# RWKV-7 attention and a SoLU layer: the mean of w_out summed at other places, and other shares of the last two inverses

## Chip, cores and metric

The kernel runs on one core of one Trainium2 chip. The metric is the device time of one execution in microseconds. A core has TensorE (PE, matrix products into PSUM), VectorE (DVE), ScalarE (ACT), GpSimd (POOL), SyncE (SP, used here only to issue DMA), and 16 DMA engines. Each engine works through its own queue in order and waits on semaphores for the others.

## What is computed

The reference is an RWKV-7 recurrence over 4 batches, 8 heads, 768 tokens and head dimension 40, followed by a SoLU layer over 3072 tokens (320 to 1024 to 320). Cut to what matters:

```python
for t in range(S):                                   # attention, per batch and head
    y[:, :, t] = einsum('bhd,bhde->bhe', rt, state)
    Sa = einsum('bhde,bhe->bhd', state, at)
    state = state * wt[:, :, None, :] - einsum('bhd,bhe->bhde', Sa, bt) + einsum('bhd,bhe->bhde', vt, kt)
h = x @ w_in                                         # x: y as (3072, 320)
solu = h * softmax(h)
ln = (solu - mean(solu)) / sqrt(var(solu) + 1e-06) * g_ln
out = ln @ w_out
```

The weights come as 64-bit floats and are turned into 32-bit floats on the chip. Instead of subtracting the mean of solu from every row, the kernel subtracts from `w_out` (with g_ln folded in, `w2`) its mean over the 1024 rows. This mean is made once.

## The kernel before

The 768 tokens are cut into 12 chunks of 64. The two batches of a pair share 128 partitions, so there are N = 24 chunks of work, numbered i. The main loop (L815) runs one pass per i, from -1 to 27; such a pass is called a slot here. A slot holds work of several chunks at once: the early part of chunk i+5 (`front`, `norm`), the recurrence of chunk i (`solved`, `read`, `leave`), the preparation of chunk i+1 (`scores`, `flip`, `couple`, `close`), and the SoLU layer of chunks i-1 to i-4 (`hidden`, `exped`, `folded`, `output`). The order of all instructions on all five engines is the order in which the Python code emits them; no scheduler moves any.

Four things matter around the change.

**The inverse.** Within a chunk the recurrence needs the inverse of a triangular matrix, made for two chunks at a time by `invert`, a generator. Inverse n serves chunks 2n and 2n+1 and is begun in slot 2n-4. It is a chain of 30 steps on VectorE, each one product (L428, `prod`) and one subtraction (L430, `uu`) over the whole of `u`. `some(k)` runs k steps; each slot calls it at four places with the numbers of `shares`, or else of a default: (3, 5, 4, 5) in even slots, (0, 5, 4, 4) in odd ones. The four places are: at the slot's start; behind `hidden(m - 2, ((0, 1),))` and ahead of `front_b`; ahead of `couple`; and behind `carried`, ahead of `leave`. In the last place the newest inverse is left alone in the slot that begins it. When the last step is done, SP writes the result to DRAM (L436, `uu_dram`), and `bring(i + 1)`, at the start of slot i, loads it for chunk i+1 into `tu` and `uh` (L449, L451).

**From inverse to coupling.** `flip` (L457) transposes `tu` on VectorE, `couple` multiplies it on TensorE (`py`), ScalarE scales the result (`wy`), `close` multiplies again (`pz`), and `read` opens `pyo`. `norm` (product `pnt`) and `answered` (product `pl`) lie between `couple` and `close`; VectorE masks their results into `nt` and `lu`, both at L375. `leave` reads `pyo` on VectorE into `x` (L619) and `tot` (L634, L636).

**PSUM.** There are three pools. `banks` (two buffers) holds, in turn, pu, ps, py, pnt, pl, pz, pyo and px of each slot (no pnt from slot 19 on), so that each of them waits until the last but one has been read: pz for nt, pyo for lu, pu for x and tot. `bank` (two buffers) holds the transposes, pcum, po and pmean. `ps2` has one buffer, `h`, for the hidden layer; in slot 2 it is used only near the end.

**The weights.** In slots -1 to 4 the weights are split from 64-bit words (`split`, L182 to L195: VectorE, then three ScalarE instructions, then VectorE). `w2` has 8 chunks of 128 rows. When chunks are there, TensorE sums them with a constant matrix of 2^-10 (`mean_of`), ScalarE copies the sum to `mean` (L231), and later calls carry it on by adding it through the identity (L227). A 128x320 product in this type is two passes of TensorE. Slot 2 sums chunks 0 to 3 and slot 3 chunks 4 and 5, both behind `spreadof`; the third sum, chunks 6 and 7, stands at the end of slot 3, and `centred` subtracts the mean in slot 4 (LAG is 1, so the code's `i == 1 + LAG` is slot 2).

Of the kernel before, what the change touches and what calls it, by code (L numbers as in the profile page):

```python
# [9 lines left out]
FP32 = mybir.dt.float32  # L10
# [7 lines left out]
P = 128  # L18
# [6 lines left out]
LAG = 1  # L25
# [23 lines left out]
def kernel(  # L49
# [18 lines left out]
    nc = tc.nc  # L68
    B, H, S, D = r.shape
    DM = H * D  # L70
    DFF = moe_w_in.shape[1]
# [13 lines left out]
    ps2 = ctx.enter_context(tc.tile_pool(name="ps2", bufs=1, space=PSUM))  # L85
# [10 lines left out]
    def c_(name):  # L96
        lo, hi = where[name]
        return cst[:, lo:hi]

    ident, tri = c_("ident"), c_("tri")  # L100
# [31 lines left out]
    w2 = const.tile([P, NF, DM], FP32, name="w2")  # L132
# [3 lines left out]
    def banks(name):  # L136
        return ps1.tile([P, 2, 512], FP32, tag="banks", name=name)

    def bank(name):
        return ps3.tile([P, 512], FP32, tag="bank", name=name)  # L140
# [56 lines left out]
    begun = []  # L197
# [23 lines left out]
            nc.scalar.mul(out=x, in_=pg[:, 0:NF], mul=2.0 ** y)  # L221


    def mean_of(lo, hi, begun=None):
        t = bank("pmean")
        if begun is not None:
            nc.tensor.matmul(t[:, 0:DM], lhsT=ident, rhs=begun, start=True, stop=False)  # L227
        for c in range(lo, hi):
            nc.tensor.matmul(t[:, 0:DM], lhsT=c_("mean"), rhs=w2[:, c, :], start=begun is None and c == lo, stop=c == hi - 1)
        mean = two.tile([P, DM], FP32, tag="osb", name="mean", bufs=1)  # L230
        nc.scalar.copy(out=mean, in_=t[:, 0:DM])  # L231
        return mean
# [7 lines left out]
    def half(p):  # L240
        return slice(C * p, C * p + C)
# [6 lines left out]
    def in_turn(tile_of, some=units):  # L248

        lots = {}  # L250
        for u in some:
            lots.setdefault(tile_of(*u), []).append(u)
        lots = list(lots.values())
        return [lot[n] for n in range(max(map(len, lots))) for lot in lots if n < len(lot)]

    def mm(o, lhsT, rhs, start=True, stop=True):
        nc.tensor.matmul(o, lhsT=lhsT, rhs=rhs, start=start, stop=stop, skip_group_check=True)  # L257
# [10 lines left out]
    def heads(ap):  # L268
        return ap.rearrange("p (h d) -> p h d", d=D)
# [13 lines left out]
    def ok(i):  # L283
        return 0 <= i < N
# [12 lines left out]
    def load_values(i):  # L297
        if not ok(i):
            return
        d = st[i]  # L300
        d["lv"] = two.tile([P, H, W2], FP32, tag="lv", name="lv", bufs=3)
        d["raw_r"] = two.tile([P, H, D], FP32, tag="raw_r", name="raw_r")
        load(d["lv"][:, :, C:], v, i)
        load(d["raw_r"], r, i, nc.gpsimd)
# [9 lines left out]
    def logged(i):  # L314
        lw = st[i]["lw"] = two.tile([P, DM], FP32, tag="lw", name="lw", bufs=1)
        nc.scalar.activation(out=lw, in_=st[i]["raw_w"].rearrange("p h d -> p (h d)"), func=AF.Ln)

    def decay(i):
        if not ok(i):
            return  # L320
        d = st[i]
        if "lw" not in d:
            logged(i)
        t = (bank("pcum") if i > 5 else ps2.tile([P, DFF], FP32, tag="h", name="h"))[:, 0:DM]
        nc.tensor.matmul(t, lhsT=c_("cum"), rhs=d["lw"], start=True, stop=True)
        nc.scalar.activation(out=ei_t[0][:, :, 0:D], in_=heads(t), func=AF.Exp)
        inv = d["inv"] = two.tile([P, DM], FP32, tag="inv", name="inv", bufs=4)
        nc.scalar.activation(out=inv, in_=t, func=AF.Exp, scale=-1.0)
# [10 lines left out]
    def turned(name, x):  # L339
        t = bank("p" + name)  # L340
        for j in range(4):
            nc.tensor.transpose(out=t[0:W2, j * P:(j + 1) * P],  # L342
                                in_=x[:, 2 * j:2 * j + 2].rearrange("p a b -> p (a b)")[:, 0:W2], identity=ident)
        return t[0:W2].rearrange("p (j b t) -> p b j t", j=4, b=2)
# [9 lines left out]
    def decay_turned(i):  # L354
        if not ok(i):
            return
        ex = st[i]["ex"] = ex_t[i % (AHEAD + 2)]
        nc.scalar.copy(out=ex[0:W2, :, :, 1:], in_=turned("ei", ei_t[0]))
# [9 lines left out]
    def front_b(i):  # L368
        if not ok(i):
            return  # L370
        d = st[i]
        d["bT"] = kept("bT", turned("b", d["kb"][:, H:]))
# [67 lines left out]
    def bring(i):  # L440
        if not ok(i):
            return
        d = st[i]
        d["tu"], d["uh"] = tu_t[i % 2], uh_t[i % 2]
        n, at = divmod(i, GRP)
        src = inverse[n].rearrange("(e a h x) c t -> e a h x c t", e=2, a=GRP, x=2)
        for x in range(2):
            queue = nc.sync if i or not x else nc.scalar
            queue.dma_start(out=d["tu"][C * x:C * x + Q, :, Q:2 * Q], in_=src[0, at, :, x].rearrange("h c t -> c h t"))  # L449
        for x in range(2):  # L450
            nc.sync.dma_start(out=d["uh"][C * x + Q:C * x + C], in_=src[1, at].rearrange("h x c t -> c (h x) t"))  # L451
# [7 lines left out]
    def couple(i):  # L459
        if not ok(i):  # L460
            return
        d = st[i]
        t = banks("py")
        for u in in_turn(lambda p, q, g, h: (p ^ h, p)):
            p, q, g, h = u
            j = 2 * q + g
            x = half(p ^ h)
            mm(t[half(p), h, j * Q:j * Q + Q], d["nt"][x, h, j], d["tu"][x, 4 * h + j, 0:Q])
        nc.scalar.activation(out=wy[:, :, :, 0:Q], in_=t[:, :, 0:4 * Q].rearrange("p h (j c) -> p h j c", j=4),  # L469
                             func=AF.Copy, scale=c_("neg_hi"))  # L470
# [170 lines left out]
    def left(i):  # L641

        if not ok(i):
            return
        x, xT = st[i]["x"], st[i]["xT"]
        for h in range(2):
            at = C * h
            nc.gpsimd.dma_start(out=xT[3 * D:P, h], in_=x[at:at + P - 3 * D, 2])
            for to in (Q * h, C + Q * h):
                nc.gpsimd.dma_start(out=xT[to:to + Q, 2], in_=x[at + P - 3 * D:at + D, 2])  # L650
# [82 lines left out]
    def some(n, kept=0):  # L733
        while len(steps) > kept and n:
            if next(steps[0], steps) is steps:
                steps.pop(0)
            else:
                n -= 1
# [72 lines left out]


    shares = {-1: (0, 2, 3, 9), 0: (4, 5, 3, 4), 1: (0, 6, 4, 5), 2: (4, 4, 3, 4), 3: (0, 5, 4, 4), 4: (6, 1, 4, 6)}
    narrowed = {-1: (0, 1, 0), 0: (0, 1, 1), 1: (1, 0, 2), 2: (0, 1, 2), 3: (1, 0, 1)}
    for i in range(-1, N + 3 + LAG):  # L815
        j, m = i + AHEAD, i - LAG
        pieces = shares.get(i, (0, 5, 4, 4) if i % GRP else (3, 5, 4, 5))
        some_weights = narrowed.get(i, (0, 0, 0))
        if i >= 1:
            bring(i + 1)  # L820
        if i >= 0:
            load_values(i + 2)
        narrow(0, pieces[0])

        solved(i)
        if i >= 0:
            scores(i + 1)
        if i >= 0:
            load_keys(j + 3, "w")
        load_keys(j + 2, "bak")  # L830

        stated(i)
        front(j)
        hidden(m - 2, ((0, 1),))
        if i == 3 + LAG:
            centred(mean)
        narrow(some_weights[1], pieces[1])
        front_b(j)
        if ok(j + 2):
            logged(j + 2)  # L840
        decay_turned(j + 1)
        hidden(m - 2, ((1, 1),))
        flip(i + 1)
        highest(m - 2)
        scaled(j + 1)
        left(i - 1)
        decay(j + 2)
        output(m - 3, 0)

        some(pieces[2])  # L850
        couple(i + 1)
        exped(m - 2)
        norm(j)
        answered(i)
        weighed(m - 2)
        spreadof(m - 2)
        if ok(j) and j % GRP == GRP - 1:
            begin_inverse(j // GRP)
        if i == 0:
            turn_g()  # L860
        if i == 1 + LAG:
            mean = mean_of(0, 4)
        if i == 2 + LAG:
            mean = mean_of(4, 6, mean)
        output(m - 3, 1)

        close(i + 1)
        read(i, True)
        carried(i + 1)
        narrow(some_weights[2], pieces[3], ok(j) and j % GRP == GRP - 1)  # L870
        by_value(i + 2)
        if ok(m - 1):
            hidden(m - 1, ((2, 0), (2, 1)))
        fence()
        read(i, False)
        driven(i + 1)
        leave(i)
        begin_narrow(narrowed.get(i + 1, (0,))[0])
        folded(m - 2)
        hidden(m - 1, ((0, 0),))  # L880
        attend_kv(i + 2)
        hidden(m - 1, ((1, 0),))
        attend_r(i + 2)
        if i == 2 + LAG:
            mean = mean_of(6, NF, mean)
# [30 lines left out]
```

## Time and profile before

| | |
|---|---|
| three runs, median | 621.12 us |
| three runs, lowest and highest | 618.76 and 623.91 us |
| profiled execution, its own time | 617.47 us |
| profiled execution, span from first to last instruction | 615.7 us |
| mean granted clock of TensorE over the span | 0.938 |
| PE, DVE, ACT, POOL busy | 547.3, 448.7, 265.6, 257.7 us |
| inverse, L430 and L428 on VectorE | 102.1 and 97.6 us, 360 instructions each |

The page names each instruction by engine, line and operation, output first ("nt<-pnt"). A timeline's row has the start and the length in microseconds, and in brackets the idle time of the engine before it, with what ended that idle time. The chain of waits follows the work back from the last instruction. PEld is the loading of weights into TensorE. In the copies quoted here, a row with "x8" stands for eight instructions merged.

By the trace, slots 2, 3 and 4 begin with pu at 108.71, 136.46 and 160.38 us. From then on a slot takes 21 to 23 us (the second half of po starts at 170.69, 193.48 and 215.02 us in slots 4, 5 and 6). Slots 17, 18, 19 and 20 have their py at 451.09, 471.76, 492.71 and 512.13 us.

### The profile page before, as it was taken

The page shows a single profiled execution, that of the slowest core. Times are in us where ns is not written, and L with a number is a line of the kernel's source. Part 1 is how long each engine was busy: PE and PEld are TensorE (multiplying, and loading weights), DVE is VectorE, ACT ScalarE, POOL GpSimd, SP SyncE. Part 2 cuts the span into 40 slices and gives each one's busy share as a digit, 9 for nine tenths or more (in the row PEclk, how much of TensorE's full clock was granted, in tenths as well). Part 3 has the DMA queues.
Part 4 walks back from the last instruction along what each step waited for, and adds up shares of the span by engine and source line. Part 5 has one row for each costly group of instructions (what it writes and reads, how often), then busy time and mean ns, then how long its engine had stood idle before and what let it go on. Part 6 is the DMA issues. An engine that isn't in the chain of part 4 may idle for free.

```text
span 615.7 us, 26656 instructions
## 1 busy us (share of the span) xinstructions
PE 547.3 (89%) x11453; PEld 397.4 (65%) x11453; DVE 448.7 (73%) x1262; ACT 265.6 (43%) x548; POOL 257.7 (42%) x424
## 2 busy tenths in 40 slices
PE   4555587689899999999999999999999999999994
PEld 3334476566576777777777677777777676676652
DVE  4797978979968869868868868688698688443431
ACT  4434455454443544454454445444433343342221
POOL 3462272472452472473365355534624631322200
PEclk9666767789999999999999999999999999999998
DMA  8986895664445454564565574564532612310100
GB/s 166 156 157 132 176 176 107 139 137 84 82 105 98 94 118 94 97 118 99 94 122 97 95 127 97 111 110 82 109 56 53 122 44 44 65 35 26 28 19 21
DMA packets 213901, 59.93 MB, mean 97 GB/s; under 512 B 199120, under 2 KB 208952, under 8 KB 213784
## 3 DMA queue, kind: packets, MB, share of 16 engines
q1 hardware_dynamic: 195512, 33.78, 32.5%
q0 software_dynamic: 11568, 19.78, 13.9%
q10 hardware_dynamic: 6704, 4.67, 2.7%
q8 instruction: 90, 1.47, 1.0%
q14 instruction: 27, 0.22, 0.1%
HBM read 40.10 MB, written 13.37 MB: 87 GB/s over the span
## 4 chain that ended last, share of the span: by engine, by line
PE 71%; DVE 15%; DMA 4%; issue 3%; ACT 3%; SPq 1%; POOL 1%; ACTq 0%; DVEq 0%; POOLq 0%
PE po L723 16%; PE h L257 15%; PE pyo L257 7%; DVE prod L428 4%; DVE uu L430 4%; PE pu L257 4%; PE plnT L712 4%; PE ps L257 3%; PE px L257 3%; PE py L257 2%; PE pl L257 2%; PE pz L257 2%; PE pst L505 2%; PE pr L342 1%; PE pei L342 1%
## 5 line engine op out<-in xcount | busy, mean ns | idle before, releaser
L257 PE MATMUL h<-w_in,xT 128*128 128x512 f32 (+1 forms) x288 | 123.0, 610 | 0.0
L723 PE MATMUL po<-w,lnT 128*128 128x320 f32 x384 | 112.7, 438 | 0.5 <-ACT lnT L713 0.5
L430 DVE TENSOR_TENSOR uu<-uu,prod 128x30 f32<-128x30 f32 (+4 forms) x360 | 102.1, 284 | 12.4
L428 DVE TENSOR_TENSOR prod<-blk,uu 128x30 f32<-128x30 f32 (+4 forms) x360 | 97.6, 271 | 9.6
L723 PEld LDWEIGHTS po<-w,lnT 128*128 128x128 f32 x384 | 71.0, 190 | 32.6 <-issue 4.1
L401 POOL DMA_DIRECT2D nt_dram<-nt x20 | 18.9, 943 | 120.0 <-DVE nt L375 98.5
L375 DVE TENSOR_TENSOR psi<-ps,cst 128x512 f32<-128x512 f32 x24 | 16.6, 690 | 66.6 <-PE ps L257 66.6
L701 POOL TENSOR_TENSOR rs<-c,mhalf 128x1 f32<-128x1 f32 x24 | 13.5, 561 | 112.1 <-DVE c L700 103.2
L650 POOL DMA_DIRECT2D xT<-x x96 | 48.7, 512 | 0.0
L257 PEld LDWEIGHTS h<-w_in,xT 128*128 128x128 f32 (+1 forms) x288 | 37.4, 189 | 9.2 <-issue 8.1
L670 DVE TENSOR_REDUCE nmax<-h 128x1 f32<-128x1024 f32 x24 | 28.6, 1193 | 18.6 <-PE h L257 18.6
L412 POOL DMA_DIRECT2D blk<-nt_dram x46 | 36.6, 802 | 10.8 <-issue 6.8
L257 PE MATMUL pyo<-lv,kb 64*64 64x104 f32 x768 | 37.8, 266 | 2.2
L257 PEld LDWEIGHTS pyo<-lv,kb 64*64 64x64 f32 x768 | 23.9, 140 | 20.9 <-issue 20.8
L638 POOL TENSOR_TENSOR st<-tot,ex 104x160 f32<-104x160 f32 x44 | 21.8, 512 | 36.6 <-DVE tot L634 23.5
L257 PE MATMUL pyo<-lu,kb 64*64 64x104 f32 x768 | 36.7, 258 | 0.0
L469 ACT ACTIVATE wy<-py,cst 128x256 f32<-128x256 f32 x24 | 11.4, 473 | 56.2 <-PE py L257 56.2
L280 POOL DMA_DIRECT2D raw_r<-in_r_dram x48 | 33.9, 709 | 0.0
L727 ACT ACTIVATE osb<-po,rs 128x320 f32<-128x320 f32 x24 | 12.7, 527 | 48.5 <-PE po L723 32.9
L554 ACT COPY x<-px 128x320 f32<-128x320 f32 x24 | 10.2, 425 | 54.1 <-PE px L257 54.0
L678 ACT ACTIVATE e<-h,nmax 128x1024 f32<-128x1024 f32 x24 | 26.6, 1108 | 14.3 <-DVE nmax L670 14.3
L684 DVE TENSOR_TENSOR e<-h,e 128x1024 f32<-128x1024 f32 x24 | 29.2, 1217 | 4.6 <-ACT e L678 4.6
(128 smaller groups left out, 1162.6 us busy)
## 6 DMA issues: line engine op xcount, KB each, us to landing
blk<-nt_dram POOLq DMA_DIRECT2D x46, 128.0 KB, 4.4
nt_dram<-nt POOLq DMA_DIRECT2D x20, 256.0 KB, 3.5
raw_w<-in_w_dram SPq DMA_DIRECT2D x48, 80.0 KB
a<-in_a_dram SPq DMA_DIRECT2D x48, 80.0 KB
raw_r<-in_r_dram POOLq DMA_DIRECT2D x48, 80.0 KB, 3.1
lv<-in_v_dram SPq DMA_DIRECT2D x48, 80.0 KB
out_dram<-osb ACTq DMA_DIRECT2D x24, 160.0 KB
raw_b<-in_b_dram SPq DMA_DIRECT2D x44, 80.0 KB
```

Of the source, the lines that this page charges most:

```text
L257: nc.tensor.matmul(o, lhsT=lhsT, rhs=rhs, start=start, stop=stop, skip_group_check=True)
L280: queue.dma_start(out=x[half(p), :, 0:D], in_=ap[2 * bp + p, :, ci * C:(ci + 1) * C, :].rearrange("h t d -> t h d"))
L412: queue.dma_start(out=nb[home:home + Q], in_=blocks[n][:, Q * e:Q * e + Q, Q * e:Q * e + Q])
L428: nc.vector.tensor_tensor(out=t, in0=nb[:, j:j + 1, j + 1:Q].to_broadcast([P, n_c, m]), in1=u[:, 0:n_c, j:j + 1].to_broadcast([P, n_c, m]) ...
L430: nc.vector.tensor_tensor(out=u[:, 0:n_c, j + 1:Q], in0=u[:, 0:n_c, j + 1:Q], in1=t, op=ALU.subtract)
L638: nc.gpsimd.tensor_tensor(out=to3(old), in0=to3(tot[0:W2]), in1=ex[:, :, 2 * q:2 * q + 2, C:].to_broadcast([W2, 2, 2, D]), op=ALU.mult)
L650: nc.gpsimd.dma_start(out=xT[to:to + Q, 2], in_=x[at + P - 3 * D:at + D, 2])
L670: nc.vector.tensor_reduce(out=nmax, in_=d["h"], axis=AX.X, op=ALU.max, negate=True)
L678: nc.scalar.activation(out=e, in_=d["h"], func=AF.Exp, bias=d["nmax"], accum_out=d["esum"])
L684: nc.vector.tensor_tensor(out=d["e"], in0=d["h"], in1=d["e"], op=ALU.mult)
L712: nc.tensor.transpose(out=t[:, j * P:(j + 1) * P], in_=d["e"][:, f * P:(f + 1) * P], identity=ident)
L723: nc.tensor.matmul(d["out"][:, 0:DM], lhsT=d["lnT"][:, f, :], rhs=w2[:, f, :], start=f == 0, stop=f == NF - 1)
```

## The change

The function `mean_of` is split in three: `mean_part` adds chunks to a given PSUM tile, `mean_kept` copies the tile to `mean`, `mean_of` carries an earlier sum on in a new tile. In slot 2 the first sum covers chunks 0 to 2 instead of 0 to 3; it is made in a tile of `h`'s pool, chunks 0 and 1 ahead of `decay_turned` (pei), chunk 2 behind `left` and ahead of `decay` (pcum), followed by the copy on ScalarE. In slot 3 the second sum covers chunks 3 to 5 instead of 4 and 5 and stands ahead of `couple` (py) instead of behind `spreadof`. The third sum (6 and 7) stays. `shares` gets entries for slots 17 to 20, the slots that hold the last two inverses, 10 and 11.

```diff
+    def mean_part(t, lo, hi, start, stop=True):
+        for c in range(lo, hi):
+            nc.tensor.matmul(t[:, 0:DM], lhsT=c_("mean"), rhs=w2[:, c, :], start=start and c == lo, stop=stop and c == hi - 1)
+
+    def mean_of(lo, hi, begun):
         t = bank("pmean")
-        if begun is not None:
-            nc.tensor.matmul(t[:, 0:DM], lhsT=ident, rhs=begun, start=True, stop=False)
-        for c in range(lo, hi):
-            nc.tensor.matmul(t[:, 0:DM], lhsT=c_("mean"), rhs=w2[:, c, :], start=begun is None and c == lo, stop=c == hi - 1)
+        nc.tensor.matmul(t[:, 0:DM], lhsT=ident, rhs=begun, start=True, stop=False)
+        mean_part(t, lo, hi, False)
+        return mean_kept(t)
+
+    def mean_kept(t):
         mean = two.tile([P, DM], FP32, tag="osb", name="mean", bufs=1)
         nc.scalar.copy(out=mean, in_=t[:, 0:DM])
         return mean
...
+    shares.update({17: (0, 6, 5, 6), 18: (5, 6, 2, 4), 19: (0, 7, 6, 6), 20: (6, 6, 4, 4)})
...
             logged(j + 2)
+        if i == 1 + LAG:
+            first = ps2.tile([P, DFF], FP32, tag="h", name="mean")
+            mean_part(first, 0, 2, True, False)
         decay_turned(j + 1)
...
         left(i - 1)
+        if i == 1 + LAG:
+            mean_part(first, 2, 3, False)
+            mean = mean_kept(first)
         decay(j + 2)
         output(m - 3, 0)

         some(pieces[2])
+        if i == 2 + LAG:
+            mean = mean_of(3, 6, mean)
         couple(i + 1)
...
-        if i == 1 + LAG:
-            mean = mean_of(0, 4)
-        if i == 2 + LAG:
-            mean = mean_of(4, 6, mean)
         output(m - 3, 1)
```

Counted on VectorE, the steps of inverse 10 done by the end of slot 17 go from 13 to 17, and its last step moves from ahead of `leave` of slot 18 to ahead of `couple` of slot 18. For inverse 11 the steps done by the end of slot 19 go from 13 to 19, and its last step moves from ahead of `leave` of slot 20 to ahead of `front_b` and `flip` of slot 20. The number of steps and of TensorE passes is the same.

More of the change, by code (lines that the diff above doesn't have):

```diff
@@ L221, in turn_g @@
             nc.scalar.mul(out=x, in_=pg[:, 0:NF], mul=2.0 ** y)
-    def mean_of(lo, hi, begun=None):
+    def mean_part(t, lo, hi, start, stop=True):
+        for c in range(lo, hi):
+            nc.tensor.matmul(t[:, 0:DM], lhsT=c_("mean"), rhs=w2[:, c, :], start=start and c == lo, stop=stop and c == hi - 1)
+    def mean_of(lo, hi, begun):
         t = bank("pmean")
-        if begun is not None:
-            nc.tensor.matmul(t[:, 0:DM], lhsT=ident, rhs=begun, start=True, stop=False)
-        for c in range(lo, hi):
-            nc.tensor.matmul(t[:, 0:DM], lhsT=c_("mean"), rhs=w2[:, c, :], start=begun is None and c == lo, stop=c == hi - 1)
+        nc.tensor.matmul(t[:, 0:DM], lhsT=ident, rhs=begun, start=True, stop=False)
+        mean_part(t, lo, hi, False)
+        return mean_kept(t)
+    def mean_kept(t):
         mean = two.tile([P, DM], FP32, tag="osb", name="mean", bufs=1)
```

## The prediction

> **What bounds the kernel now.** I read the busy tenths first: TensorE (PE) is at 8 or 9 from the tenth slice on, VectorE (DVE) leads before that. The chain of waits agrees: PE holds 71% of it, DVE 15%. So time counts where TensorE waits, or where the VectorE chain of the first 156 us passes. Whose waits they are comes from the table of waits from 166 us on; the rest from the timelines of slots 2, 3 (108 to 162 us) and 17 to 20 (444 to 516 us), and from the busy time by stretch, which has the granted clock.
>
> ```profile
> PE   4555587689899999999999999999999999999994
> DVE  4797978979968869868868868688698688443431
> PE 71%; DVE 15%; DMA 4%; issue 3%; ACT 3%; SPq 1%; POOL 1%; ACTq 0%; DVEq 0%; POOLq 0%
> ```
>
> From 166 us on TensorE waits twice for `flip`:
>
> ```profile
> PE py L257 <- DVE tu L457: 1.6, 2, 1.2
> ```
>
> Slot 2, in order of time (start, length, instruction, idle before it in brackets):
>
> ```profile
> 119.08 0.44 DVE L457 STREAM_TRANSPOSE tu<-tu 128x256 f32<-128x256 f32 x1
> 122.34 4.48 PE L229 MATMUL pmean<-w,cst 128*128 128x320 f32 x8
> 126.75 0.67 PE L257 MATMUL pz<-uh,wy 64*64 64x32 f32 x32
> 127.49 0.37 ACT L481 COPY tu<-pz 128x256 f32<-128x256 f32 x1 [0.20 <-PE pz L257]
> 128.95 0.49 DVE L193 SCALAR_TENSOR_TENSOR bits<-bits,scale 128x320 int32<-128x320 int32 x1 [2.09 <-ACT scale L185]
> 132.17 0.76 DVE L619 TENSOR_TENSOR x<-pyo,ex 104x256 f32<-104x256 f32 x2
> ```
>
> The mean holds pz 4.4 us, pz holds ScalarE (ACT), and ScalarE holds VectorE 2.09 us. Before that, TensorE stood idle 1.38 us ahead of pei (115.07) and 2.16 us ahead of pcum (117.88).
>
> Slots 18 to 20:
>
> ```profile
> 466.43 0.69 DVE L375 TENSOR_TENSOR psi<-ps,cst 128x512 f32<-128x512 f32 x1 [2.35 <-PE ps L257]
> 471.26 0.44 DVE L457 STREAM_TRANSPOSE tu<-tu 128x256 f32<-128x256 f32 x1
> 492.12 0.45 DVE L457 STREAM_TRANSPOSE tu<-tu 128x256 f32<-128x256 f32 x1 [0.79 <-DMA tu<-uu_dram]
> 492.71 0.67 PE L257 MATMUL py<-tu,nt 64*64 64x32 f32 x32 [1.18 <-DVE tu L457]
> 495.78 0.68 DVE L375 TENSOR_TENSOR lu<-pl,cst 128x512 f32<-128x512 f32 x1
> 496.64 0.67 PE L257 MATMUL pyo<-rT,s 40*64 40x64 f32 x32
> 512.13 0.67 PE L257 MATMUL py<-tu,nt 64*64 64x32 f32 x32 [0.43 <-DVE tu L457]
> ```
>
> The reader is to see how thin the cover is: in slot 19 the transfer makes flip only 0.79 us late after five steps, and lu (ending 496.46) is just in time for pyo.
>
> **The Trainium skill.** "TensorE: Matmul & The Clock Gate", Part 1: The HAM clock gate, says an idle TensorE falls to half clock. The trace agrees in size: granted clock 0.53 from 120 to 127 us, mean passes 0.55 us each (4.41/8), against 0.27 at the third sum (159.37). "SBUF — State Buffer", SBUF: two separate sides, says VectorE with two SBUF inputs and GpSimd (POOL) lock one port pair against each other. The trace fits: one step at 119.68 took 2.17 us instead of 0.27 while GpSimd multiplied kb (120.05 to 121.74).
>
> **Part 1, the mean.** The passes are the same 20 (8 chunks and 2 carried sums, two passes each); none is added. Only places change.
>
> Slot 2: four passes between pb and pei. pb ends 113.69 and 4 x 0.27 = 1.1 us fits the 1.38 idle. Two more fit ahead of pcum, which waits for lw; the mean's copy (0.43) on ScalarE runs while it awaits pcum (idle 1.05). At half clock the first four take 2.2 us, making pei 0.8 us late; pcum still waits for lw. So this placing costs 0. It borrows h's bank, idle until the first h (129.01). Then pz waits no longer for the mean, but for nt, whose PSUM bank it reuses: nt ends 123.53, so pz 123.59 instead of 126.75. ScalarE follows 3.16 us sooner; VectorE's own queue ends 126.86, so L193 starts then, and x (L619), 3.22 us of contiguous work later, at 130.1 instead of 132.17: **2.1 us** (ScalarE's two results are there by 125.75 and 127.35, pyo by 128.0, so neither takes over). ScalarE's next scale waits for VectorE, kT for ScalarE, pr for kT, so slot 3 shifts by the same 2.1.
>
> GpSimd shifts less: its issues end 131.67, then one bits issue (0.57), so st starts about 132.3 instead of 133.34. If VectorE gets caught behind it, 1.0 us of the gain remains; I take 2.1, since psi waits for TensorE anyway.
>
> Slot 3: carried sum and three chunks (8 x 0.27 = 2.2 us) stand ahead of py where only 1.17 was idle, so py is 1.0 late. Behind it on TensorE queue pnt, pl, pz; on ScalarE the mean's copy delays wy and e. Cover: pnt ends 145.04, nt starts 147.04 (2.0 spare); pl has 1.8, e (ACT ends 146.2, used 148.24) 2.0. About 0.9 of each is left: cost 0, and 1.4 us of mean ahead of pz go for nothing, as pz waits for nt. The third sum stays.
>
> Part 1 carries through slot 3 (VectorE frees lnT, TensorE resumes 156.40): **-2.1**, bounds -3.2 (pz's whole shift) and 0.
>
> **Part 2, the steps.** No step is added. A step, two instructions, takes from its row to the next step's row: 0.45 for the first, 0.52 and 0.58 for the sixth and seventh, 0.60 to 0.65 for the tenth to nineteenth, then falling to 0.40 for the last. Inverse 10 has 17 steps done by the end of slot 17 (before 13), and all 30 ahead of nt in slot 18; inverse 11 has 19 in slot 19 (before 13), and all ahead of flip in slot 20. So its uu_dram transfer leaves about 6.5 us sooner (475 instead of 481.56), and flip's 0.79 wait goes. SP issues nothing more; its xT issues follow x. But every step stands ahead of a VectorE instruction that TensorE waits for: py needs flip (0.59 later in slot 19's rows), pz reuses nt's bank where there is an nt, pyo reuses lu's. Slot 3 shows both: nt ends 147.72, pz 147.78; lu ends 148.32, pyo 148.38. Replaying the rows, lateness against before:
>
> - Slot 17: a sixth step before flip, +0.52: py 451.27, was 451.09. Two more before lu: +1.24, lu ends 456.33, pyo 456.39 instead of 455.82: **0.57**. Then six steps instead of four: x at 463.4, was 460.79; SP's xT and the tu load behind them land 471.6, just in time.
> - Slot 18: five steps instead of three ahead of psi, which starts 467.8 (TensorE allows 467.0); six, smaller, behind it: flip 472.66, py 473.25 instead of 471.76: **1.49**. The 2.35 idle is used up. lu is on time, x follows pyo.
> - Slot 19: psi follows TensorE (+1.49). Seven steps instead of five, +1.1, so flip 493.84, py 494.43: **1.72**; the transfer's wait has become a wait for steps. Thirteen instead of nine before lu, which ends 499.6: pyo 499.65 instead of 496.64: **3.01**.
> - Slot 20: six steps both before and after x push psi to 511.4, five more flip to 514.86, py 515.45: **3.3**. From there TensorE bounds (slots 21 on), and nothing wins it back.
>
> So +3.3, though the two waits, 1.6, are gone. Bounds: -1.6 (no new wait) and +4.5 (tu landing late in slots 18 and 20, 0.6 each).
>
> **Sum.** -2.1 + 3.3 = +1.2. The profiled execution has a span of 615.7 and took 617.47 (1.8 around it), below the three runs' lowest, 618.76. The sum is a difference, so on the median 621.12 it gives **622.3 us**; its own range 619.5 to 625.5. A measurement can tell about 1%, 6.2 us.
>
> **Rivals.**
> - Fewer waits alone: lu and flip keep ahead of TensorE, e.g. if steps shorten. -2.1 - 1.6 = -3.7: 617.4. For it: VectorE idles 2.35 and 4.10 us ahead of psi. Against: those gaps lie before psi, the steps behind it.
> - Half clock: without the 4.4 us mean TensorE stays cold, and slot 3's eight passes take 4.4 us. py at 145.0, pnt 146.3, nt due at 145.0: 1.3 late, so 0.8 of the gain is left, more lost in slot 2: 624. For: clock 0.53 there. Against: 1.0 from 127 us, and TensorE is busy from pz on. It decides above 0.4 us a pass.
> - Port lock, the slower side: steps moved beside GpSimd's st, raw_r and xT issues each get caught as at 119.68, 1.9 us a slot, now on TensorE's path. Four slots: +7.6, 630. Against: in slots 17 and 19 steps beside st took 0.42 instead of 0.29, and kb's products are over by slot 18. From three such blocks on it passes 1%.
> - Not done: excluded, the compiled order shows each move.
>
> **How the numbers follow.** Forecast 0.57, fewer waits 0.21, half clock 0.14, port lock 0.08. The range 616.5 to 626.5 takes in the first three, leaving out the lock and the outer edges. Faster by over 1% (below 614.9) needs more than both gains at once: 0.06. Slower by over 1% (above 627.3) is the lock: 0.09. Within 1%: 0.85.
>
> **What would show it.** Right: in slot 2 no 2.09 us ahead of L193; TensorE out of the early stages about 2 us sooner; new waits of pyo for lu in slots 17 and 19 (0.4 and 1.3 us), of py for flip in slots 18 to 20, none for tu's transfer. Wrong: no such waits, or VectorE steps of 2 us.

## The result, and the profile after

| | before | changed |
|---|---|---|
| median of 22 runs | 620.98 us | 623.73 us |
| lowest and highest | 617.76, 624.86 | 620.30, 628.35 |
| ratio, 95% interval | 1 | 1.0043 [1.0025, 1.0061] |
| profiled execution, span | 615.7 us | 622.2 us |

The changed kernel is slower by 0.43%, some 2.7 us (1.6 to 3.8 by the interval). The two profiled executions differ by 6.5 us, so more than half of their difference is chance, and the traces have to be read by stages. The page of the changed kernel, busy tenths and chain of waits:

```profile
PE   4445568798999999999999999899999899999994
PE 66%; DVE 23%; issue 4%; ACT 3%; DMA 2%; POOL 1%; ACTq 1%; DVEq 0%; SPq 0%; POOLq 0%
```

TensorE's row has new eights late in its full part, and VectorE's share of the chain of waits went from 15% to 23%. The table of waits of TensorE from 166 us on (total, times, longest) says where:

```profile
PE ps L262 <- issue: 4.0, 3, 1.8
PE py L262 <- DVE tu L462: 3.2, 3, 1.4
PE pyo L262 <- DVE lu L380: 1.1, 1, 1.1
PE pz L262 <- DVE nt L380: 0.3, 1, 0.3
```

Before, the second line was 1.6 in two waits, and the last two were absent. The first line is another thing: TensorE stops in the middle of a row of products, and this view names nothing that it waits for ("issue"). It was there before too (1.5, 2 times). Such a stop is called a gap from here on; the last section says what was found of it.

The waits in order of time, from TensorE's timeline:

```profile
475.17 0.67 PE L262 MATMUL py<-tu,nt 64*64 64x32 f32 x32 [0.90 <-DVE tu L462]
491.21 0.58 PE L262 MATMUL ps<-rT,vT 40*64 40x64 f32 x24 [1.06 <-issue]
497.66 0.67 PE L262 MATMUL py<-tu,nt 64*64 64x32 f32 x32 [1.42 <-DVE tu L462]
502.85 0.69 PE L262 MATMUL pyo<-rT,s 40*64 40x64 f32 x32 [1.09 <-DVE lu L380]
518.66 0.67 PE L262 MATMUL py<-tu,nt 64*64 64x32 f32 x32 [0.89 <-DVE tu L462]
```

These are slots 18, 19 (three rows) and 20; in slot 17 pz waited 0.29 us for nt. In slot 19 flip no longer waits for a transfer (its row in VectorE's timeline has no idle time), and in all three slots py waits for flip because of the steps queued ahead of it:

```profile
497.07 0.44 DVE L462 STREAM_TRANSPOSE tu<-tu 128x256 f32<-128x256 f32 x1
```

Slot 2, VectorE's timeline: the 2.09 us ahead of L193 are gone, and x now waits a little for TensorE.

```profile
128.36 0.48 DVE L193 SCALAR_TENSOR_TENSOR bits<-bits,scale 128x320 int32<-128x320 int32 x1
131.38 0.75 DVE L624 TENSOR_TENSOR x<-pyo,ex 104x256 f32<-104x256 f32 x2 [0.15 <-PE pyo L262]
```

The next table takes differences between the starts of py of the slots, in us. The start of the kernel is left out of it, since py of slot -1 moves by up to 3.6 us between the executions traced here. Every row is one traced execution; e4, e5, e6 and e11 were run only once, so that they stand on their trace alone.

| execution | slot 2 to 4 | 4 to 16 | 16 to 20 | gap in slot 19 |
|---|---|---|---|---|
| before | 49.15 | 261.29 | 82.11 | none |
| changed | 46.75 | 264.18 | 86.56 | 1.06 |
| changed, again (e11) | 48.42 | 264.49 | 86.59 | 1.06 |
| e1, mean alone | 48.61 | 263.23 | 82.15 | none |
| e2, shares alone | 48.09 | 261.65 | 85.29 | none |
| e3, mean and idle shares | 47.94 | 261.75 | 81.19 | 0.61 |
| e10, the same again | 46.73 | 261.77 | 81.73 | 1.16 |
| e8, idle shares alone | 48.38 | 262.39 | 81.43 | 0.89 |
| e4, shares of inverse 10 | 47.74 | 261.82 | 83.68 | 0.87 |
| e5, shares of inverse 11 | 48.67 | 265.44 | 83.93 | none |
| e6, slot 3's sum put back | 46.74 | 262.33 | 83.98 | none |
| e7, warmed | 46.59 | 263.22 | 82.46 | 1.79 |
| e9, chunk 3 in the wait | 48.55 | 262.98 | 83.59 | 1.44 |

Slots 4 to 16 run the same instructions in all of them and still scatter by 4 us: there TensorE stops in slots 5 and 15 in the middle of ps, and in some executions ScalarE is late once or the clock drops after a stop. That is the chance in a single trace. It reaches into the last columns too. e6 has the old shares, as before has, and its 83.98 is 1.9 us more than before's 82.11: its wait in slot 19 is 0.3 us longer (1.50), and behind it the clock is 0.50 for 3.4 us, in which the eight po products take 3.96 us instead of 2.42. In e9 the same follows the gap of 1.44 us: without the gap slots 16 to 20 take 82.2 us there, against 80.6 in e3, which has the same shares.

### The profile page after: what moved, and what is told of

Read it like the earlier page. It is cut to its first block, busy times and chain, and to the rows that moved or that the text cites. A ratio compares the mean times of both kernels' runs of the same rounds, so it can differ in the third digit from the quotient of the medians.

```text
span 622.2 us, 26656 instructions
## 1 busy us (share of the span) xinstructions
PE 547.9 (88%) x11453; PEld 398.9 (64%) x11453; DVE 449.1 (72%) x1262; ACT 265.6 (43%) x548; POOL 257.5 (41%) x424
## 3 DMA queue, kind: packets, MB, share of 16 engines
q8 instruction: 90, 1.47, 1.0%
## 4 chain that ended last, share of the span: by engine, by line
PE 66%; DVE 23%; issue 4%; ACT 3%; DMA 2%; POOL 1%; ACTq 1%; DVEq 0%; SPq 0%; POOLq 0%
PE po L728 15%; PE h L262 14%; DVE uu L435 7%; PE pyo L262 7%; DVE prod L433 6%; PE plnT L717 3%; PE pu L262 3%; PE ps L262 3%; PE px L262 3%; PE py L262 2%; PE pl L262 2%; PE pz L262 2%; PE pst L510 2%; PE pr L347 1%; PE pei L347 1%
## 5 line engine op out<-in xcount | busy, mean ns | idle before, releaser
L262 PE MATMUL h<-w_in,xT 128*128 128x512 f32 (+1 forms) x288 | 124.5, 617 | 0.0
L435 DVE TENSOR_TENSOR uu<-uu,prod 128x30 f32<-128x30 f32 (+4 forms) x360 | 105.7, 294 | 12.4
L433 DVE TENSOR_TENSOR prod<-blk,uu 128x30 f32<-128x30 f32 (+4 forms) x360 | 95.3, 265 | 9.7
L559 ACT COPY x<-px 128x320 f32<-128x320 f32 x24 | 10.2, 425 | 56.9 <-PE px L262 56.8
L732 ACT ACTIVATE osb<-po,rs 128x320 f32<-128x320 f32 x24 | 12.7, 527 | 48.5 <-PE po L728 32.9
## 6 DMA issues: line engine op xcount, KB each, us to landing
blk<-nt_dram POOLq DMA_DIRECT2D x46, 128.0 KB, 4.4
```

Of the source, the lines that this page charges most:

```text
L433: nc.vector.tensor_tensor(out=t, in0=nb[:, j:j + 1, j + 1:Q].to_broadcast([P, n_c, m]), in1=u[:, 0:n_c, j:j + 1].to_broadcast([P, n_c, m]) ...
L435: nc.vector.tensor_tensor(out=u[:, 0:n_c, j + 1:Q], in0=u[:, 0:n_c, j + 1:Q], in1=t, op=ALU.subtract)
```

## The experiments

**e1, the mean alone, and e2, the shares alone.** The edits:

```diff
-    shares.update({17: (0, 6, 5, 6), 18: (5, 6, 2, 4), 19: (0, 7, 6, 6), 20: (6, 6, 4, 4)})
```

taken from the changed kernel gives e1; the same line added to the kernel before gives e2.

> The mean moved, the old shares kept. Theory (steps late for flip and lu cost 3.3 us, the mean gains): ratio to the kernel before about 0.996, 2.1 to 2.4 us faster; no 2.09 us of idle ahead of L193 in slot 2; TensorE's waits for flip in slots 19 and 20 (1.2 and 0.4 us) stay, no wait of pyo for lu. Rival (half clock, the mean gains nothing or loses): 1.000 or above, and the loss of the changed kernel is in the early slots.

> The new shares, the mean left where it was. Theory: slots 17 to 20 come out 3.3 us longer than before (py of slot 20 against py of slot 16), ratio about 1.0055; new waits of py for flip in slots 18 to 20 and of pyo for lu in slots 17 and 19. Rival (the shares only take the two waits away, and the changed kernel's loss is gaps in TensorE's instruction supply): 1.6 us faster, ratio 0.9975.

Measured: e1 ratio 0.9995 [0.9973, 1.0017], e2 ratio 1.0064 [1.0039, 1.0088]. So the loss is the shares', 4.0 us (2.4 to 5.5), and by the trace 85.29 - 82.11 = 3.2 us of it lie in slots 16 to 20, with no gap among them. TensorE's waits in e2 from 166 us on are those of the changed kernel:

```profile
PE py L257 <- DVE tu L457: 3.2, 3, 1.4
PE pyo L257 <- DVE lu L375: 1.1, 1, 1.1
PE pz L257 <- DVE nt L375: 0.3, 1, 0.3
```

The rival that the shares only take waits away falls. The mean brought 0.3 us (1.7 gain to 1.1 loss) instead of 2.1: the expectation for e1 missed. VectorE's timeline of slot 2 in e1:

```profile
120.48 0.49 DVE L193 SCALAR_TENSOR_TENSOR bits<-bits,scale 128x320 int32<-128x320 int32 x1
129.59 0.48 DVE L193 SCALAR_TENSOR_TENSOR bits<-bits,scale 128x320 int32<-128x320 int32 x1
134.39 0.76 DVE L624 TENSOR_TENSOR x<-pyo,ex 104x256 f32<-104x256 f32 x2 [1.95 <-PE pyo L262]
```

L193 is as early as forecast, and then x loses 1.95 us to a new wait, for pyo. Why pyo is late is in TensorE's timeline of e1:

```profile
126.38 1.08 PE L262 MATMUL pz<-uh,wy 64*64 64x32 f32 x32 [1.18 <-DVE nt L380]
127.25 1.11 PE L262 MATMUL pyo<-rT,s 40*64 40x64 f32 x32
130.50 2.08 PE L262 MATMUL h<-w_in,xT 64*128 64x512 f32 x4
```

Before, these rows took 0.67, 0.67 and 1.13 us. In e1 TensorE is at half clock. The busy time by stretch in e1 (stretch, its length, busy time and count of PE, PEld, DVE, ACT, POOL, then granted clock, DMA share, GB/s):

```profile
122.00:126.00 4.00, 2.84 (x96) 2.65 (x96) 3.83 (x8) 1.07 (x3) 3.74 (x6) 0.50 0.87 177
126.00:130.00 4.00, 3.62 (x116) 3.62 (x120) 3.76 (x16) 2.41 (x6) 3.14 (x7) 0.50 0.63 127
130.00:134.00 4.00, 3.91 (x60) 2.26 (x56) 2.38 (x6) 1.80 (x4) 2.63 (x4) 0.50 0.65 123
```

and before, in the last two of these stretches:

```profile
126.00:130.00 4.00, 4.00 (x134) 2.55 (x133) 1.75 (x6) 2.87 (x7) 1.82 (x4) 0.93 0.71 131
130.00:134.00 4.00, 3.91 (x78) 2.77 (x76) 3.73 (x11) 2.44 (x6) 2.91 (x5) 1.00 0.70 153
```

Before, the clock came back by 127 us, at the end of the mean's 4.4 us. In e1 it is still 0.50 at 134.

The trace of before was itself an unlucky draw for the forecast. e2 leaves the mean where it was, and there the clock came back during the mean:

```profile
125.45 3.43 PE L229 MATMUL pmean<-w,cst 128*128 128x320 f32 x8
131.01 0.49 DVE L193 SCALAR_TENSOR_TENSOR bits<-bits,scale 128x320 int32<-128x320 int32 x1 [1.02 <-ACT scale L185]
```

The mean took 3.43 us instead of 4.48, and VectorE waited 1.02 us ahead of L193 instead of 2.09. In e8, the third trace with the mean in its old place, it was 3.51 and 1.12. From py of slot 2 to x it took 12.59 us before, 11.55 in e2 and 11.63 in e8. With the mean moved it is 10.2 us in the changed kernel's first trace, e10 and e6, where pz and pyo run at full clock, and 10.9 to 12.0 in e1, e3, e4, e5 and e11, where they run at half. So against e2 and e8 the move gains 1.4 us when TensorE is at full clock, and loses 0.4 when it is at half clock for longest.

**e7, the same with TensorE kept busy.** To e3 (below), ten passes are added whose sums nobody reads, in places where TensorE waits:

```diff
             mean_part(first, 2, 3, False)
+            for c in (0, 1):
+                mm(first[:, 512:512 + DM], c_("mean"), w2[:, c, :])
             mean = mean_kept(first)
...
         answered(i)
+        if i == 1 + LAG:
+            for c in (0, 1, 2):
+                mm(first[:, 512:512 + DM], c_("mean"), w2[:, c, :])
```

> The kernel of e3_idle_shares with ten more passes on TensorE in slot 2 whose sums nobody reads: four ahead of pcum and six between pl and pz, where it waits anyway. Theory (the mean's gain is eaten because TensorE, now without the 4.4 us of mean, runs slot 2 at half clock and x then waits for pyo): clock at least 0.85 from 123 to 132 us after the shift of the start, x at most 0.3 us behind the last w product, L193 of chunk 3 to x (L624) 12.1 us as in the changed kernel's profile, against 13.2 in e3_idle_shares; ratio to before about 0.9945. Rival (the clock follows something else): x still 0.6 us or more late and the ratio as e3_idle_shares or above, since ten passes were added.

In the trace of e7 the clock is 1.00 from 114 to 134 us and x does not wait:

```profile
122.00:126.00 4.00, 3.66 (x108) 2.59 (x102) 3.86 (x9) 0.46 (x2) 4.00 (x8) 1.00 0.93 195
126.00:130.00 4.00, 3.91 (x160) 3.04 (x155) 3.73 (x16) 3.93 (x9) 1.96 (x4) 1.00 0.39 86
131.28 0.76 DVE L624 TENSOR_TENSOR x<-pyo,ex 104x256 f32<-104x256 f32 x2
```

From L193 of chunk 3 (119.31) to x it took 11.97 us, the shortest of all (12.1 in the changed kernel's first trace, 13.9 in e1, 14.5 before), and slot 2 to 4 took 46.59. That agrees with the theory, but it is one trace, and three kernels without the added passes came within 0.2 us of it when the clock happened to stay up; so it does not show that the added passes are what kept the clock up. The expected ratio was missed: 0.9985 [0.9965, 1.0005]. That interval neither excludes no change nor the ratios of e3. In its trace TensorE's gaps are longer in sum than elsewhere (1.27, 0.71, 1.07, 1.79 us, 4.8 together), which may hide the gain; this was not settled.

**e9, chunk 3 summed in the wait ahead of pz.**

```diff
-            mean_part(first, 2, 3, False)
-            mean = mean_kept(first)
+            mean_part(first, 2, 3, False, False)
...
         answered(i)
+        if i == 1 + LAG:
+            mean_part(first, 3, 4, False)
+            mean = mean_kept(first)
```

with the second sum then over chunks 4 and 5.

> The kernel of e3_idle_shares with chunk 3 summed in slot 2 between pl and pz (two passes where TensorE waits 1.0 to 2.0 us for nt), so that slot 3 sums chunks 4 and 5 only. Theory: costs nothing (two passes are 0.5 us at full and 1.1 us at half clock, inside the wait) and hardly warms TensorE, so x still waits for pyo by what the clock of slot 2 makes of it; ratio as e3_idle_shares, within 0.002. Rival (more work in the wait keeps the clock up): x no more than 0.3 us late, 0.002 faster.

Ratio 0.9978 [0.9955, 1.0002]; x waited 1.94 us for pyo, the clock was 0.50 from 126 to 130 us. In this trace two passes did not keep TensorE at full clock, as the theory had it.

**e6, slot 3's sum put back behind spreadof.**

```diff
-        if i == 2 + LAG:
-            mean = mean_of(3, 6, mean)
         couple(i + 1)
...
+        if i == 2 + LAG:
+            mean = mean_of(3, 6, mean)
         output(m - 3, 1)
```

> The mean alone moved, old shares, and slot 3's sum (chunks 3 to 5) put back behind spreadof, where before had chunks 4 and 5. Theory (slot 3's place is covered both ways): from py of slot 2 to pk at slot 3's end within 0.3 us of the mean-only kernel at the same clock in slot 2; pz of slot 3 waits for nt less or not at all. Rival (the place ahead of py is what costs the mean's gain): 1 us or more less from py of slot 2 to pk.

From py of slot 2 (119.72) to pk at slot 3's end (154.14) it took 34.42 us. In the first trace of the changed kernel, with the clock about as high, 155.59 - 121.17 = 34.42. So, by one trace each, the place of slot 3's sum is worth nothing either way, and pz waits for nt in the changed kernel (1.01 us) and not in e6.

**e4 and e5, the new shares of one inverse.** The mean moved, with only `17: (0, 6, 5, 6), 18: (5, 6, 2, 4)` in e4 and only `19: (0, 7, 6, 6), 20: (6, 6, 4, 4)` in e5.

> The mean moved, new shares for slots 17 and 18 (inverse 10) alone. Theory, replaying the rows of before: py of slot 17 +0.2, of slot 18 +1.5, of slot 19 +0.55 and of slot 20 +0.55 us against slot 16's py (the wait for the transfer in slot 19 takes up the rest), the 0.43 us wait in slot 20 stays. Rival (lateness adds up slot by slot whatever follows): +1.5 or more still there in slot 20.

> The mean moved, new shares for slots 19 and 20 (inverse 11) alone. Theory, replaying the rows of before: py of slot 19 +0.2 (the transfer's wait is still there), pyo of slot 19 late for lu by about 1.3 us, py of slot 20 +1.8 us against slot 16's py. Rival (the loss comes from inverse 10, which crowds VectorE first): +0.5 or less.

e4, lateness of py against before, counted from slot 16: +0.1, +1.3, then +1.6 in slots 19 and 20, of which 0.87 is the gap, so 0.7 without it (0.55 expected). The 0.43 us wait in slot 20 stayed (0.44). e5: +0.25 in slot 19, +1.8 in slot 20, as expected; pyo waited 1.08 us for lu. Both together cost more (3.4 without the gap, or 3.2 in e2) than 0.7 + 1.8. The reason is the wait for the transfer in slot 19, which each fills alone: in e4 TensorE's lateness fills it, in e5 the two more steps ahead of flip do (flip has no idle time ahead of it there, so that in this point the expectation missed). Together there is only one such wait to fill.

**e3 and e10, the steps put where VectorE idles.**

```diff
-    shares.update({17: (0, 6, 5, 6), 18: (5, 6, 2, 4), 19: (0, 7, 6, 6), 20: (6, 6, 4, 4)})
+    shares.update({18: (6, 5, 4, 5), 19: (0, 4, 5, 4), 20: (5, 4, 4, 4)})
```

> The mean moved, and the steps that are moved sooner go only where VectorE idles ahead of psi: shares 18: (6, 5, 4, 5), 19: (0, 4, 5, 4), 20: (5, 4, 4, 4). Theory: flip is ready before TensorE in slots 19 and 20, no wait of py or pyo from slot 16 on is over 0.2 us, so 1.6 us less than with the old shares and 3.7 to 4.0 us less than before, ratio 0.994. Rival (any earlier step costs as much as it brings, since VectorE has no spare time in these slots): like the mean alone, 0.996 to 0.997.

> The kernel of e3_idle_shares once more, for its size and beside e9_chunk3_wait. Theory: 0.994 to 0.998, so that with the first reading (0.9966) it is faster than before for certain. Rival (e3_idle_shares was a lucky draw, the mean's move and the idle shares are worth nothing each): 0.999 to 1.001.

Ratios 0.9966 [0.9947, 0.9985] and 0.9983 [0.9960, 1.0006]. The first interval lies below 1, the second includes no change; both exclude a loss of 0.1%. The waits for flip, nt and lu are all gone; what is left of TensorE's waits from 420 to 530 us in e3 is one line:

```profile
PE ps L262 <- issue: 0.6, 1, 0.6
```

Without that gap slot 16 to 20 takes 80.6 us in e3, e10 and e8, 1.5 us less than before: three more steps ahead of psi in slot 18 and two in slot 20 fit the idle time there, and one less ahead of flip in slots 19 and 20 lets flip be ready in time. It is the only version here with a reading that is clear of no change against the kernel before, and it has the lowest medians (619.56 and 619.44 us).

**e8, the idle shares alone,** on the kernel before.

> The kernel before with the idle shares alone, the mean left where it was. Theory: the 1.6 us of waits in slots 19 and 20 go and nothing else changes, ratio 0.9975; py of slot 20 80.6 us after py of slot 16 (82.1 before). If the mean's move is worth nothing on average, this is as fast as e3_idle_shares (0.9966); if it is worth its 2.1 us, 0.0035 slower.

Ratio 0.9998 [0.9977, 1.0019]. The waits went as expected (81.43 us, or 80.54 without the gap), but the time did not follow by 1.6 us: 0.89 of it was given back as a gap in slot 19, and the rest lies within the interval. Against e3 it leaves 2.0 us for the mean's move, against e10, the same kernel, 0.9; the changed kernel against e2 leaves 1.3, and e1 against before 0.3. Together they do not fix the mean's worth better than that it lies between 0 and about 2 us.

**e11, the changed kernel once more.**

> The changed kernel once more, for a second trace. Theory: the waits of slots 17 to 20 are the same to 0.1 us (pz 0.3, py 0.9, 1.4 and 0.9, pyo 1.1), while x in slot 2 waits for pyo by anything from 0 to 2 us by the clock there, and the gap of TensorE's instruction supply in slot 19 is there again with another length. Rival: the gap in slot 19 was an accident of one execution and is not there.

Here x waited 1.82 us in slot 2 (0.15 in the first trace), the clock was 0.50 there from 126 to 130 us. pz waited 0.29 and py 0.91 and 1.42 as in the first trace. The wait of pyo for lu in slot 19, expected at 1.1 us, was missing, and py of slot 20 waited 0.33 us instead of 0.89. The reason is in TensorE's timeline: behind py of slot 19 the clock was 0.50 for 3.4 us, the eight po products took 4.11 us instead of 2.42, and lu was ready meanwhile. The waits were filled, not saved: from slot 19 to slot 20 it took 21.0 us in both. The gap in slot 19 was 1.06 us again.

## Why the prediction was right, and where it was off

The direction was right, and +2.7 us measured against +1.2 forecast lies within the range. But the closeness is in part luck: the forecast is the sum of one term that was right and one that was too large, and a third, the gap in slot 19, was not in it.

**The steps (+3.3) were right, one by one.** From py of slot 16 on, against before, and without the gap: slot 17 py +0.10 (0.18 forecast), pyo +0.56 (0.57); slot 18 py +1.33 (1.49); slot 19 py +1.81 (1.72), pyo +3.07 (3.01); slot 20 py +3.39 (3.3). One of the waits forecast was another: in slot 17 it was pz that waited, for nt (0.29), and pyo came late behind it. Then nothing is won back: slots 20 to 22 take 37.82 us in both. What carried it were the two rules read off slot 3's rows (pz follows nt, pyo follows lu) and the 0.59 us from flip to py. The rival of fewer waits alone is refuted by e2. Its observation, that VectorE idles ahead of psi, was sound all the same, and e3 makes use of it. The rival of the port lock did not come about: in slots 17 to 20 no instruction of a step takes over 0.45 us in the traces of the changed kernel and of e2.

**The mean (-2.1) was mis-sized.** The mechanism was right in its first half: L193 came 2.2 us sooner after py of slot 2 than before. The step that failed is "ScalarE's two results are there by 125.75 and 127.35, pyo by 128.0, so neither takes over": it used pyo's durations at full clock, and in five of the eight traces pz and pyo ran at half clock, and x started 0.6 to 1.8 us later after py of slot 2 than in the other three. The second half of the error is that 2.09 us was read from one execution; e2 and e8 had only 1.02 and 1.12 us to win. In slot 2 to 4 the eight traces with the mean moved (e7 and e9 left out) took 46.73 to 48.67 us, 47.7 on average, the three without it 48.09 to 49.15, 48.5 on average; so the move brings about 0.8 us, in single executions 2.4 or nothing, and by e1's timing 0.3. In slots 4 to 16, which hold the same instructions, the same eight took 263.1 us on average and the three 261.8; whether that is chance or a cost that the move has later on, so few traces do not tell.

Of the half clock rival, the cause fits (TensorE without the 4.4 us of mean often stays at half clock in slot 2) and the place was wrong in the main: it put its sized loss into slot 3's passes, which ran at 0.27 us each, and it was x in slot 2 that waited for pyo, which the rival has only as "more lost in slot 2". The argument against it, that the clock is 1.0 from 127 us, took from the trace of before what the removed work may itself have brought about: with the mean in place pz ran at full clock in three traces of three, without it in three of eight. The costing of both new places at nothing was right: py of slot 1 to py of slot 2 takes 20.84 to 20.97 us in all thirteen traces, and e6 shows it for slot 3.

**What was missing** is the gap in slot 19, 1.06 us in both traces of the changed kernel, absent before. By the traces that makes -0.8 + 3.4 + 1.1 = +3.7, which lies within the 1.6 to 3.8 of the timing, near its upper end.

**The start.** py of slot -1 comes at 56.9 to 60.5 us in these traces, in kernels with the same instructions up to there, so no difference between two single spans of this kernel under some 4 us can be laid to an edit.

## What to carry to other kernels

Where an engine's queue is in order, work moved sooner delays everything behind it: count the idle time in front of each place, and put steps only ahead of an instruction that waits for another engine anyway. A block of matrix work that looks like mere delay may be what brings TensorE back to full clock; when it is moved off the path, cost what follows it at half clock too. Read a wait from several executions before counting on it: the one ahead of L193 was 2.09, 1.12 and 1.02 us in three. Time a part alone when the whole is a sum of a gain and a loss.

## What the runs showed of the hardware that was not expected

**The gaps.** TensorE stops at fixed places of its program: after 25 of 32 products of ps in slots 5 and 15, for 0.5 to 1.8 us, in every kernel with the same number of TensorE instructions. In e7, with ten more passes, the stops of slots 5 and 15 are at other products of ps. The page of both kernels lists a DMA queue of the kind "instruction" with 90 packets, 1.47 MB together, so 16 KB each:

```profile
q8 instruction: 90, 1.47, 1.0%
```

Set beside these packets, all 26 stops of slots 5 and 15 in the thirteen traces end 1.3 to 1.9 us after such a packet has ended. So TensorE seems to wait there for its next instructions. The stop in slot 19 is there in eight of the nine traces in which inverse 10 was done sooner (e2 is the exception; in e7 it is at another product) and in none of the four in which it was not. It ends 1.5 to 1.7 us after a packet too. Where it is there, that packet starts 12.4 to 13.6 us after py of slot 18; in the other five traces the packet of this place starts 9.8 to 10.5 us after it, in time. What makes it start later when inverse 10 is done sooner was not found.

**The clock.** The granted clock falls to 0.5 after short pauses (none over 1.62 us ahead of the fall in e1), and can stay there while TensorE is busy. Every stretch at half clock that begins after 100 us and ahead of the last 20 us lasts, in all thirteen traces, 3.41, 6.83, 10.24 or 13.65 us, that is 1, 2, 3 or 4 times 3.41. The Trainium skill, "TensorE: Matmul & The Clock Gate", Part 1: The HAM clock gate, gives about 3.4 us of activity for the return, of a window that runs freely. The traces agree with the length. Cut at such borders, TensorE in e1 (stretch, its length, busy time and count of PE, granted clock, DMA share, GB/s):

```profile
117.61:121.02 3.41, 1.54 (x7) 1.00 0.61 97
127.85:131.26 3.41, 3.41 (x86) 0.50 0.45 100
131.26:134.67 3.41, 3.32 (x60) 0.50 0.76 153
134.67:138.08 3.41, 3.10 (x32) 1.00 0.86 183
```

The clock fell after a stretch that was 1.54 us busy (1.27 before, 1.36 in the changed kernel). It came back after a stretch busy for 3.32 us, but not after the one ahead of it, which was busy throughout with 86 mostly small products; before, a stretch with 98 products, all but two of them small (119.71 to 123.13 us), did not bring it back either, and the next, full of the mean's passes, did. What the clock counts as activity these runs do not show, and the page does not explain it. Where such a border falls against the kernel's own work differs from one execution to the next, which fits x being 0.15 or 1.82 us late in the same kernel.

In slots 16 to 20 a pause of TensorE of 1.42 to 1.50 us was followed by 3.41 us at half clock in e6, e9 and e11, and pauses of 1.42 to 1.79 us were not in the changed kernel's first trace, e2, e5 and e7. So a wait of that length can cost about twice what the table of waits says, as in e6, or not, by chance.
